# Even classes of a folded token transform folded once more: two 256x256 matrices in place of one 512x512, in a spectral filter block with its gradients

## The chip, the cores and the metric

The kernel runs on one core of a Trainium2 chip. The metric is the device time of one execution in microseconds (us). Engines are called by the profile's names: PE is TensorE (matmul, and PEld its weight loads), DVE is VectorE, ACT is ScalarE, POOL is GpSimd, SP is SyncE, which issues transfers. The chip has fast working memory in 128 partitions (SBUF), accumulators that matmuls write (PSUM), and main memory (DRAM here).

## The reference: what is computed

One block of a network on x of 2048 tokens by 1024 channels, conditioned by a vector c, and all gradients of it for a given grad_out. In short:

```
mod = silu(c) @ w_mod                 # six rows: sa, ca, ga, sb, cb, gb
h   = layernorm(x) * (1 + ca) + sa
x   = x + ga * irfft2(rfft2(h) * (w_r + 1j * w_i))       # A
h   = layernorm(x) * (1 + cb) + sb
n   = layernorm(h)
x   = x + gb * (gelu_tanh(n @ w1 + b1) @ w2 + b2)        # B, 1024 -> 3584 -> 1024
```

A is a filter over both the token axis and the channel axis. Its gradient is a transform, a product with the conjugate weights and a transform back once more, so the program holds two spectral passes: one forward, one backward. The outputs are x and the gradients for x, w_r, w_i, w1, b1, w2, b2, c and w_mod.

## The kernel before, in words

**Transforms as matmuls.** A real transform of 2048 tokens is computed with cosine and sine matrices after folding. A chunk i (of four) holds four groups of 128 tokens: rows 128i and 1024 + 128i are loaded in order, their mirror images, 2047 - 128i and 1023 - 128i downwards, by row indices through POOL (`load_tok`, L126). `fold_tok` (L271) adds and subtracts the mirrored groups on DVE, which gives four classes: even and odd cosine (CE, CO), even and odd sine (SE, SO), each with 512 rows over the four chunks and a 512x512 matrix. `fold_d` (L260) does the same along the channels. `unfold_tok` (L288) and `unfold_d` (L277) undo it. All these are additions through one helper, `tt` (L173), so in the profile they stand on L173.

**One spectral pass** is `spectral_core` (L478), called forward at L742 and backward at L1309. Its stages:

- `s_fwd` (L467) for CE, SE, CO, SO: eight column tiles of a class, four matmuls each (128x128 weights, 512 moving columns, L472), evicted from PSUM to U by a copy (L647; forward either ACT or DVE as the scheduler chooses). The matrices of CE and SE are in tile smA, those of CO and SO in smB.
- eight `pair`s (L495): the transform along channels (matmuls pcs of 256 columns, L505), the product with w_r and w_i on DVE, into R.
- `s_inv` (L556): back along the token frequencies, again four matmuls of 512 columns for each of eight tiles of a class (pv, L565), evicted to V. CE and SE run after the sixth pair, CO and SO after the eighth; CE and SE use a matrix tile smi.
- four chunks: 32 matmuls po of 256 columns each (L630), eight to a class, evicted into o4, a part of the tile ct (L635, L637), then `consume` of this chunk.

`consume_fwd` (L726) unfolds the chunk, stores it (d_A), adds the gated result to x, normalizes twice and stores the normalized rows (d_n, L740) from its temporary, ct[:,1] for even chunks and ct[:,2] for odd ones. ct has four such parts. `consume_bwd` (L1184) unfolds, forms the layernorm's gradient and column sums (accCA), and writes the gradient of x.

**What runs beside it.** PE has other matmuls to fill the gaps. Forward it is `ph_part` (L678, L684): grad_out times w2 transposed, 896 matmuls pp of 512 columns in 14 groups, each group with a weight tile wt that SP transposes while loading (L301; two in turn). grad_out is transposed for it by PE (pt, L344) and evicted with a column sum (L347 DVE, L351 ACT); the result pho is evicted (L691, L694) and stored. After that come `z_block` (n times w1, pz, L802; gelu and its derivative on ACT and DVE into tiles hh), which loads the normalized rows transposed as n3T (L791), and `bo_pass` (hh times w2, pbo, L853). Then `pg_pass` (L950), the layernorm gradients, and the second fold, `fold_quarter` (L1094). Beside the backward pass run the gradients of w2 (gw2acc, L1075, which loads hh again) and, at the end, of w1 (gw1acc, L1266).

**What sets the order.** A scheduler that knows the dependences fixes one order per engine when the program is built. On the chip each engine goes through its list and waits where an operand is not there. Evictions have a raised priority (`tc.high_priority`), some instructions are bound behind others (`issue_after`), and z_block and bo_pass follow a plan list. PSUM is divided by tags: "s" with 2 buffers (pu, pv, half of po and pcs), "d" for the other half, "f" with 4 (pt, pp and the gradients).

SP carries, in the stretch after the forward transform, the loads of wt, the stores of d_n, the loads of x (xt) and of n3T, and then w1 and hh, one after another.

## Time and profile before

| what | value |
|---|---|
| median of three runs | 1461.49 us (1461.4 to 1465.73) |
| profiled execution: its own time | 1459.13 us |
| its span | 1457.3 us |
| mean granted PE clock | 0.992 |
| ACT busy | 752.2 us, 52% |
| POOL busy | 366.1 us, 25% |

The stretches of the span that the change touches, by the busy time of the engines in the trace:

| stretch, us | what PE does | PE | DVE | ACT |
|---|---|---|---|---|
| 0 to 128 | conditioning rows, transposes, first pp | 98.95 | 99.03 | 76.87 |
| 128 to 156 | s_fwd, forward | 27.68 | 0.96 | 18.61 |
| 190 to 206 | s_inv of CE and SE, pairs 7 and 8 | 15.60 | 13.58 | 11.05 |
| 218 to 231 | s_inv of CO and SO | 13.00 | 1.10 | 8.24 |
| 231 to 272 | po of chunks 0 to 2, pp | 39.11 | 39.22 | 26.61 |
| 1020 to 1049 | s_fwd, backward | 29.00 | 11.12 | 19.31 |
| 1144 to 1159 | s_inv of CE and SE | 15.00 | 11.74 | 9.32 |
| 1189 to 1206 | s_inv of CO and SO | 15.22 | 7.15 | 9.54 |
| 1206 to 1353 | po, consume, gw2 and gw1 beside | 142.61 | 133.97 | 63.89 |

How to read the profile: a group of instructions has the line of the kernel, engine, operation, output<-input tiles, partitions x elements with type and the count; behind the first bar the busy time in us and the mean of one in ns; behind the second the idle time of the engine just before them, and what ended it. A line of a timeline has start and length in us, then the same, with the idle time before it and its releaser in brackets. Matmuls overlap, so the mean of one is longer than the distance from one to the next; the distance is read from a timeline, by start times and counts.

The longest waits of PE were for the weight blocks of the conditioning rows (12.4 us over six times, all before 100 us), for the eviction of the transposes (4.6), for evictions of po (3.9 on ACT, 1.1 on DVE), for R in s_inv (3.0) and for a wt tile (2.6, once).

### The profile page before, as it was taken

To read this page: it belongs to the slowest core of one execution; us is meant where nothing else is said; L and a number is where in the kernel's file an instruction comes from. 1 tells how busy PE (TensorE), PEld (TensorE's weight loads), DVE (VectorE), ACT (ScalarE), POOL (GpSimd) and SP (SyncE) were. 2 spreads that over 40 slices of the span, in tenths; PEclk is the share of its full clock that TensorE was granted. 3 is DMA by queue.
4 is the path that set the end of the run, shared out by engine and by line. 5 is a ranking of instruction groups with operands and counts; after the bars stand their busy time and mean duration, and the time that the engine had idled before them with its cause. 6 is when DMAs were issued, how large, how long until landed. Compare 5 with 4: busy or idle time off the path is not lost. (4 is left out here: it accounts for less than half of the span.)

```text
span 1457.3 us, 18411 instructions
## 1 busy us (share of the span) xinstructions
PE 1396.5 (96%) x6835; PEld 649.0 (45%) x6835; DVE 1058.4 (73%) x1483; ACT 752.2 (52%) x1065; POOL 366.1 (25%) x441
## 2 busy tenths in 40 slices
PE   5889999999999999999999999999999999999997
...
GB/s 333 286 214 70 142 235 115 270 255 337 257 203 278 259 250 233 201 264 241 277 297 245 74 271 185 107 270 176 181 217 254 254 233 213 194 191 180 297 279 65
DMA packets 358367, 324.28 MB, mean 223 GB/s; under 512 B 209386, under 2 KB 301056, under 8 KB 358022
## 3 DMA queue, kind: packets, MB, share of 16 engines
...
## 5 line engine op out<-in xcount | busy, mean ns | idle before, releaser
L684 PE MATMUL pp<-gBoT,wt 128*128 128x512 bf16 x896 | 197.9, 380 | 4.5 <-DMA wt<-in_B_w_dram 2.6
L950 PE MATMUL pg<-w1T,gzr 128*128 128x512 bf16 x896 | 197.1, 381 | 0.2 <-ACT gn3b L961 0.2
L1266 PE MATMUL gw1acc<-gzh,n3n 128*128 128x512 bf16 x896 | 195.4, 379 | 1.3 <-DMA gzh<-d_gz 1.3
L684 PEld LDWEIGHTS <-wt 128*128 128x128 bf16 x896 | 87.7, 98 | 109.4 <-issue 4.2
L950 PEld LDWEIGHTS <-gzr 128*128 128x128 bf16 x896 | 87.3, 98 | 108.7 <-issue 6.6
L802 PEld LDWEIGHTS <-w 128*128 128x128 bf16 x896 | 87.3, 98 | 108.8 <-issue 4.7
L1266 PEld LDWEIGHTS <-n3n 128*128 128x128 bf16 x896 | 87.4, 98 | 106.1 <-issue 2.7
L802 PE MATMUL pz<-n3Tb,w 128*128 128x512 bf16 x448 | 99.2, 379 | 1.6 <-DVE w2sD L875 1.4
L802 PE MATMUL pz<-n3Ta,w 128*128 128x512 bf16 x448 | 98.7, 379 | 1.1 <-ACT gt L805 1.1
L1075 PE MATMUL gw2acc<-gB,hhsA 128*128 128x512 bf16 x448 | 98.5, 379 | 1.0 <-DMA hhsA<-d_hh 1.0
L853 PEld LDWEIGHTS <-hhA 128*128 128x128 bf16 x608 | 59.0, 98 | 71.7 <-issue 1.4
L805 ACT ACTIVATE gt<-pz,b_col 128x512 bf16<-128x512 f32 x112 | 72.5, 684 | 34.2 <-PE pz L802 32.8
L1270 ACT CAST gwo<-gw1acc 128x512 bf16<-128x512 f32 x50 | 29.1, 583 | 113.6 <-PE gw1acc L1266 99.0
L173 DVE TENSOR_TENSOR gt<-gt,gt 128x2048 bf16<-128x2048 bf16 x56 | 68.3, 1223 | 22.4 <-ACT gt L813 21.2
L1082 ACT CAST gwo<-gw2acc 128x512 bf16<-128x512 f32 x46 | 26.7, 583 | 109.9 <-PE gw2acc L1075 75.6
L811 ACT ACTIVATE gt<-gt 128x2048 bf16<-128x2048 bf16 x28 | 53.5, 1910 | 55.7 <-DVE gt L173 55.7
L173 DVE TENSOR_TENSOR ct<-ct 128x2048 bf16<-128x2048 bf16 x64 | 75.9, 1218 | 1.8 <-DMA d_n<-ct 1.1
L1075 PEld LDWEIGHTS <-hhsA 128*128 128x128 bf16 x448 | 43.6, 98 | 53.0 <-DMA hhsA<-d_hh 1.7
L997 DVE CUSTOM_DVE_ANT_0 otl<-otl 128x1024 bf16<-128x1024 bf16 x24 | 29.1, 1223 | 49.9 <-DMA otl<-in_w_mod_dram 44.2
L807 ACT ACTIVATE gt<-gt 128x2048 bf16<-128x2048 bf16 x28 | 53.4, 1908 | 5.4 <-DVE hhC L173 2.5
L813 ACT ACTIVATE gt<-gt 128x2048 bf16<-128x2048 bf16 x28 | 53.5, 1909 | 0.5
L1271 POOL DMA_DIRECT2D out_dram<-gwo x56 | 30.6, 548 | 85.6 <-ACT gwo L1270 53.4
...
## 6 DMA issues: line engine op xcount, KB each, us to landing
...
```

The lines of the kernel that those rows point to most:

```text
L173: return nc.vector.tensor_tensor(out=out, in0=a, in1=b, op=op)
L684: last_pe[0] = nc.tensor.matmul(pp[:], lhsT=wt[:, fg % 2, cch, k * P:(k + 1) * P], rhs=gBoT[j][:, cch, :], start=(cch == 0), stop=(cch == ...
L802: last_pe[0] = nc.tensor.matmul(pz[:], lhsT=w1s[g][:, cch, k * P:(k + 1) * P], rhs=n3T[:, cch, :], start=(cch == 0), stop=(cch == NDC - 1))
L805: nc.scalar.activation(out=zb[:, k, :], in_=pz[:], func=ACT.Identity, bias=b1_col[:, fc:fc + 1], scale=1.0)
L807: nc.scalar.activation(out=av, in_=zb, func=ACT.Square)
L811: nc.scalar.activation(out=sg, in_=bv, func=ACT.Sigmoid, scale=2.0 * GK)
L813: nc.scalar.activation(out=bv, in_=bv, func=ACT.Sigmoid, scale=-2.0 * GK)
L853: last_pe[0] = nc.tensor.matmul(pbs[i][:], lhsT=hh[:, k, i * P:(i + 1) * P], rhs=wp[:, k, :], start=False, stop=(g == 6 and k == 3))
L950: last_pg[0] = nc.tensor.matmul(pgs[i][:], lhsT=gzs[b, g][:, k, i * P:(i + 1) * P], rhs=w1Ts[g][:, k, h * KH:(h + 1) * KH], start=(g == 0 ...
L1075: nc.tensor.matmul(acc[:], lhsT=hh_of(fc)[:, t, :], rhs=gBs[t // 4][:, t % 4, h * KH:(h + 1) * KH], start=(t == 0), stop=(t == NT - 1))
L1266: nc.tensor.matmul(acc[:], lhsT=n3ns[t // 4][:, t % 4, cch * P:(cch + 1) * P], rhs=gz2[t // 8][:, t % 8, :], start=(t == 0), stop=(t == NT ...
L1271: nc.gpsimd.dma_start(out=out_4[cch * P:(cch + 1) * P, fg * 512:(fg + 1) * 512], in_=ob)
```

## The change

The even classes are folded a second time over tokens. Chunk 2j + 1 no longer holds the tokens after those of chunk 2j but their mirror images about a quarter of the axis: rows 512 + 128j and 1536 + 128j in order, 511 - 128j and 1535 - 128j downwards by index (`tok_rows`, `tok_plain`, `tok_idx`). For the even classes, chunks 2j and 2j + 1 are added and subtracted (`fold_pair`, in place of `fold_d` in odd chunks). The sum needs only every other frequency, the difference the rest, so the 512x512 matrix of an even class becomes two of 256x256. The frequencies are ordered so that they stay apart: in s_fwd and s_inv each tile of CE and SE has two halves of 256 columns with two matmuls of 256 columns each, where it had four of 512 columns. CO and SO stay as they were, with their rows in the new order.

On the way back po of an even chunk takes both halves of the even classes for itself and for the odd chunk behind it: 48 matmuls and 12 evictions (16 matmuls for CO and SO, 32 for the halves), and the odd chunk 16 matmuls and four evictions, for CO and SO alone. The halves go to a tile eb; DVE adds them into this chunk's o4 and subtracts them into the next one's. Forward eb is ct[:, 1 + i % 2]; backward it is a tile of its own.

Besides: matrices, their generation and their copies in DRAM (d_SF, d_SI) become smaller for the even classes, smi takes four transposing loads instead of eight; w_r and w_i rows and their gradients follow the new order of frequencies with the same number of transfers; the transposes of grad_out become matmuls against the identity or a reversed identity with results in fp32, so that the reversal at pho's eviction goes; the row sa (saf) is added in odd chunks only, with factor 8 for 4; the column sum sacc takes a copy and an addition instead of a copy and three; backward all evictions of U, cs and V are ACT's, and PSUM tiles of the even classes there alternate between tags "s" and "f". The number of matmuls is 6835 before and after.

The diff, cut to its core:

```diff
@@ -123,45 +126,55 @@
     def tok_flat(ap):
         return ap[0] if len(ap.shape) == 3 else ap
 
+    def tok_rows(s3, i, lo, n):
+        step, base = (1024, 128 * (i // 2)) if i % 2 == 0 else (-1024, 1536 + 128 * (i // 2))
+        return bass.AP(tensor=s3.tensor, offset=s3.offset + base * D + lo, ap=[[D, P], [step * D, 2], [1, n]])
+
+    def tok_plain(t4, i):
+        return t4[:, 0:4:3, :] if i % 2 == 0 else t4[:, 1:3, :]
+
+    def tok_idx(i, q):
+        return 1 + q if i % 2 == 0 else 3 * q
+
     def load_tok(t4, src, i, eng=None):
         s3 = tok_flat(src)
-        ins = (eng or nc.sync).dma_start(out=t4[:, 0:4:3, :],
-                          in_=bass.AP(tensor=s3.tensor, offset=s3.offset + 128 * i * D, ap=[[D, P], [1024 * D, 2], [1, D]]))
+        ins = (eng or nc.sync).dma_start(out=tok_plain(t4, i), in_=tok_rows(s3, i, 0, D))
         for q in range(2):
-            nc.gpsimd.indirect_dma_start(out=t4[:, 1 + q, :], out_offset=None, in_=s3,
+            nc.gpsimd.indirect_dma_start(out=t4[:, tok_idx(i, q), :], out_offset=None, in_=s3,
...
@@ -267,6 +283,20 @@
         dv = dst.rearrange("p c (a b w) -> p c a b w", b=2, w=256)
         tt(dv[:, :, :, 0, :], tv[:, :, :, 0, :], tv[:, :, :, 1, :], ALU.add)
         return tt(dv[:, :, :, 1, :], tv[:, :, :, 0, :], tv[:, :, :, 1, :], ALU.subtract)
+
+    def fold_pair(dst, prev, src, tmp, spare):
+        n = 4
+        fwd = src.rearrange("p c (b w) -> p c b w", w=512)[:, :, :, 0:256]
+        rev = bass.AP(tensor=src.tensor, offset=src.offset + 1023, ap=[src.ap[0], [D, n], [-512, 2], [-1, 256]])
+        tv = tmp.rearrange("p c (s b w) -> p c s b w", s=2, w=256)
+        tt(tv[:, :, 0], fwd, rev, ALU.add)
+        tt(tv[:, :, 1], fwd, rev, ALU.subtract)
+        for c0, out in ((0, spare), (1, dst[:, 1:4:2, :])):
+            dv = out.rearrange("p c (a b w) -> p c a b w", b=2, w=256)
+            tt(dv[:, :, :, 0, :], tv[:, c0:4:2, :, 0, :], tv[:, c0:4:2, :, 1, :], ALU.add)
+            tt(dv[:, :, :, 1, :], tv[:, c0:4:2, :, 0, :], tv[:, c0:4:2, :, 1, :], ALU.subtract)
+        tt(dst[:, 0:4:2, :], prev[:, 0:4:2, :], spare, ALU.subtract)
+        return tt(prev[:, 0:4:2, :], prev[:, 0:4:2, :], spare, ALU.add)
 
     def fold_tok(h4, tmp):
...
@@ -339,9 +369,11 @@
         nc.vector.tensor_copy(out=gb_col[:], in_=pc[:, 0:NDC])
     for j in range(4):
         for cch in range(NDC):
-            pt = psum.tile([P, BW], BF16, tag="f", name="pt", bufs=4)
+            pt = ps_f("pt")
             for a in range(4):
-                nc.tensor.transpose(pt[:, a * P:(a + 1) * P], gos[j][:, a, cch * P:(cch + 1) * P], ident[:])
+                q = (0, 2, 3, 1)[a] if j % 2 == 0 else (1, 3, 2, 0)[a]
+                nc.tensor.matmul(pt[:, q * P:(q + 1) * P], lhsT=gos[j][:, a, cch * P:(cch + 1) * P], rhs=(ident, irev)[a // 2],
+                                 start=True, stop=True)
             if cch % 2 == 0:
                 with tc.high_priority():
...
@@ -467,10 +506,16 @@
     def s_fwd(cl, fb, sm, evac):
         Ut = reg.tile([P, 8, 512], BF16, name=f"U{cl}", tag=f"uv{cl}")
         for c8 in range(8):
-            pu = ps_s("pu")
-            for i in range(4):
+            pu = (ps_f if cl % 2 == 0 and c8 % 2 and fb is not fbuf else ps_s)("pu")
+            for i in range(4 if cl % 2 else 0):
                 last_pu[0] = nc.tensor.matmul(pu[:], lhsT=fb[:, i, cl, c8 * P:(c8 + 1) * P], rhs=sm[:, i, :],
                                               start=(i == 0), stop=(i == 3))
+            for k in range(0 if cl % 2 else 2):
+                cols = slice(k * 256, (k + 1) * 256)
+                for j in range(2):
+                    i = 2 * j + (k if cl == CE else 1 - k)
+                    last_pu[0] = nc.tensor.matmul(pu[:, cols], lhsT=fb[:, i, cl, c8 * P:(c8 + 1) * P], rhs=sm[:, j, cols],
+                                                  start=(j == 0), stop=(j == 1))
             with tc.high_priority():
                 evac(Ut[:, c8, :], pu[:])
...
@@ -560,10 +607,12 @@
                 dc, h = c8 // 2, c8 % 2
                 k0 = (0, 1, 2, 1)[dc] + 256 * h
                 base = k0 + (PW if (dc >= 2) == (cl < 2) else 0)
-                pv = ps_s("pv")
+                pv = (ps_f if cl % 2 == 0 and c8 % 2 and not fwd else ps_s)("pv")
                 for m in range(4):
-                    nc.tensor.matmul(pv[:], lhsT=R[:, cl * 4 + m, :, :].rearrange("p x w -> p (x w)")[:, base:base + 255:2],
-                                     rhs=smi[:, cl // 2, m, :], start=(m == 0), stop=(m == 3))
+                    k = (m // 2 + cl // 2) % 2
+                    out, m0, m1 = (pv[:], 0, 3) if cl % 2 else (pv[:, k * 256:(k + 1) * 256], m // 2 * 2, m // 2 * 2 + 1)
+                    nc.tensor.matmul(out, lhsT=R[:, cl * 4 + m, :, :].rearrange("p x w -> p (x w)")[:, base:base + 255:2],
+                                     rhs=smi[:, cl // 2, m, :], start=(m == m0), stop=(m == m1))
                 with tc.high_priority():
                     evac_v(Vt[:, c8, :], pv[:])
 
@@ -575,11 +624,11 @@
         smis = []
 
         def load_smi():
-            smi = reg.tile([P, 2, 4, 512], BF16, name="smi", tag="sma")
+            smi = reg.tile([P, 2, 4, 256], BF16, name="smi", tag="sma")
             for t in range(2):
                 with tc.issue_after(ld_in[0].ins):
                     if fwd:
-                        for i in range(4):
+                        for i in range(2):
                             nc.sync.dma_start_transpose(out=smi[:, t, :, i * P:(i + 1) * P], in_=d_SF[:, 2 * t, i, :])
                     else:
...
@@ -618,24 +667,34 @@
             nc.vector.tensor_scalar(out=gm[:, 8:12, :], in0=gm[:, 4:8, :], scalar1=-1.0, scalar2=None, op0=ALU.mult)
         ct = reg.tile([P, 4, 4, D], BF16, name="ct", tag=o4tag)
         xts = [reg.tile([P, 4, D], BF16, name="xt", tag=tg)[:] for tg in ("sma", "smb" if fwd else "px0")]
+        eb = None if fwd else reg.tile([P, 4, D], BF16, name="eb", tag="smb")[:]
         for i in range(4):
-            o4 = ct[:, 3 * (i % 2)]
-            for cl in range(4):
+            o4, on = ct[:, 3 * (i % 2)], ct[:, 3 - 3 * (i % 2)]
+            if fwd:
+                eb = ct[:, 1 + i % 2]
+            half = [(cl, eb[:, 2 * k + cl // 2], k * 256 + i // 2 * P) for cl in (CE, SE) for k in range(2)]
+            for cl, ov4, c0 in (half if i % 2 == 0 else []) + [(cl, o4[:, cl], i * P) for cl in (CO, SO)]:
                 for hh_ in range(2):
                     po = (ps_d, ps_s)[hh_]("po")
                     for d2 in range(2):
                         dc = 2 * hh_ + d2
                         for h in range(2):
                             gi = 2 * dc + h + (4 if (dc >= 2 and cl >= 2) else 0)
-                            nc.tensor.matmul(po[:, d2 * 256:(d2 + 1) * 256], lhsT=Vs[cl][:, 2 * dc + h, i * P:(i + 1) * P],
+                            nc.tensor.matmul(po[:, d2 * 256:(d2 + 1) * 256], lhsT=Vs[cl][:, 2 * dc + h, c0:c0 + P],
                                              rhs=gm[:, gi, :], start=(h == 0), stop=(h == 1))
                     with tc.high_priority():
-                        ov = o4[:, cl, hh_ * 512:(hh_ + 1) * 512]
+                        ov = ov4[:, hh_ * 512:(hh_ + 1) * 512]
                         if fwd or (cl, hh_) != (3, 0):
                             nc.any.tensor_copy(out=ov, in_=po[:])
                         else:
                             last_po[0] = nc.scalar.copy(out=ov, in_=po[:])
-            consume(i, o4, ct[:, 1 + i % 2], ct[:, 2 - i % 2], xts[i % 2])
+            if i % 2 == 0:
+                tt(o4[:, 0:4:2, :], eb[:, 0:2, :], eb[:, 2:4, :], ALU.add)
+                if fwd:
+                    tt(on[:, 0:4:2, :], eb[:, 0:2, :], eb[:, 2:4, :], ALU.subtract)
+            elif not fwd:
+                tt(o4[:, 0:4:2, :], eb[:, 0:2, :], eb[:, 2:4, :], ALU.subtract)
+            consume(i, o4, ct[:, 1 + i % 2], ct[:, 2 - i % 2], xts[i % 2], eb)
 
     def new_pair_temps(tags):
...
@@ -686,12 +745,8 @@
             q = (0, 2, 3, 1)[j]
             ov = ph2[:, :, q * P:(q + 1) * P]
             pv = pp[:, :].rearrange("p (i w) -> p i w", w=P)
-            if j % 2 == 0:
-                with tc.high_priority():
-                    nc.any.tensor_copy(out=ov, in_=pv)
-            else:
-                with tc.high_priority():
-                    nc.any.tensor_copy(out=ov, in_=bass.AP(tensor=pv.tensor, offset=pv.offset + 511, ap=[pv.ap[0], [-P, 4], [-1, P]]))
+            with tc.high_priority():
+                nc.any.tensor_copy(out=ov, in_=pv)
         if js[-1] == 3:
             nc.gpsimd.dma_start(out=d_ph[fc * P:(fc + 1) * P, :], in_=ph2.rearrange("p i w -> p (i w)"))
...
@@ -718,12 +773,16 @@
         norm_act(fb, x4, 0, i)
         tt(fb, fb, bcn(opca_row, 4), ALU.mult)
         fold_tok(fb, x4)
-        fold_d(fb, fb, x4[:])
-        tt(fb[:, 0, :], fb[:, 0, :], saf, ALU.add)
+        if i % 2 == 0:
+            fold_d(fb, fb, x4[:])
+        else:
+            pv_ = fbuf[:, i - 1]
+            fold_pair(fb, pv_, fb, x4[:], x4s[i - 1][:, 0:2, :])
+            tt(pv_[:, 0, :], pv_[:, 0, :], saf, ALU.add)
     css = reg.tile([P, 2, 2, 2 * PW], BF16, name="cs01", tag="px0")
     nc.gpsimd.memset(css[:], 0.0)
 
-    def consume_fwd(i, o4, tmp, tmp2, x4):
+    def consume_fwd(i, o4, tmp, tmp2, x4, eb):
         unfold_d(o4, tmp)
         unfold_tok(o4, tmp)
...
@@ -1093,7 +1152,10 @@
 
     def fold_quarter(b, ftmp, g2):
         fold_tok(ftmp, g2)
-        fold2_in[b] = fold_d(fbuf2[:, b], ftmp, g2)
+        if b % 2 == 0:
+            fold2_in[b] = fold_d(fbuf2[:, b], ftmp, g2)
+        else:
+            fold2_in[b] = fold_pair(fbuf2[:, b], fbuf2[:, b - 1], ftmp, g2, ftmp[:, 0:2, :])
 
     for b in range(NB):
...
@@ -1181,12 +1243,12 @@
     nc.gpsimd.memset(css2[:], 0.0)
     accCA = []
 
-    def consume_bwd(i, o4, tmp, tmp2, n1):
+    def consume_bwd(i, o4, tmp, tmp2, n1, eb):
         if i == 0:
             accCA.append(ps_s("accCA"))
-            nc.vector.tensor_copy(out=sacc, in_=o4[:, 0, :])
-        else:
-            tt(sacc, sacc, o4[:, 0, :], ALU.add)
+            nc.vector.tensor_copy(out=sacc, in_=eb[:, 0, :])
+        elif i == 2:
+            tt(sacc, sacc, eb[:, 0, :], ALU.add)
         unfold_d(o4, tmp)
         unfold_tok(o4, tmp)
...
@@ -1307,14 +1369,14 @@
                     next(rows34)
 
     spectral_core(False, fbuf2, (smA2, smB2), em2, [css2[:, 0], css2[:, 1]],
-                  new_pair_temps(["t0", "t1", "t2", "t3"]), act_copy, s_copy, act_copy, consume_bwd, "fr", pfs, fill, mid_bwd, beside_bwd)
+                  new_pair_temps(["t0", "t1", "t2", "t3"]), s_copy, s_copy, s_copy, consume_bwd, "fr", pfs, fill, mid_bwd, beside_bwd)
 
 
     accSA = [ps_d("accSA0"), ps_d("accSA1")]
     colsum(accSA, sacc, True, True)
...
```

## The prediction

> **What bounds the kernel now.** I read the page's busy shares first, then the groups of instructions of the even classes, then TensorE's waits, then the timelines of the four stages that the change touches.
>
> ```profile
> PE 1396.5 (96%) x6835; PEld 649.0 (45%) x6835; DVE 1058.4 (73%) x1483; ACT 752.2 (52%) x1065; POOL 366.1 (25%) x441
> ```
>
> TensorE (PE) is busy for 96% of the span: time taken from its stream is gained unless a wait takes its place. The even classes are two groups, with their weight loads and a group of half-width matmuls beside them:
>
> ```profile
> L472 PE MATMUL pu<-smA,fbuf 128*128 128x512 bf16 x128 | 28.5, 379 | 0.6 <-DVE fbuf L173 0.6
> L565 PE MATMUL pv<-smi,R 128*128 128x512 bf16 x128 | 28.4, 379 | 1.4 <-DVE R L173 1.2 <-ACT V L647 0.2
> L472 PEld LDWEIGHTS <-fbuf 128*128 128x128 bf16 x256 | 24.9, 98 | 31.4 <-DVE fbuf L173 1.1 <-issue 0.6
> L505 PE MATMUL pcs<-empf,U 128*128 128x256 bf16 x128 | 15.3, 273 | 0.0
> ```
>
> The 379 ns of one matmul is latency, not spacing. Spacing comes from PE's timeline at the start of the backward transform:
>
> ```profile
> 1018.64 2.11 PE L1075 MATMUL gw2acc<-gB,hht 128*128 128x512 bf16 x9
> 1020.58 14.00 PE L472 MATMUL pu<-smA,fbuf 128*128 128x512 bf16 x64
> 1034.51 0.61 PE L196 MATMUL acc3b<-au,ones_bf 128*32 128x512 bf16 x8
> 1048.88 1.91 PE L505 MATMUL pcs<-empf,U 128*128 128x256 bf16 x16
> 1050.63 0.59 PE L1075 MATMUL gw2acc<-gB,hhsA 128*128 128x512 bf16 x2
> ```
>
> (34.51 - 20.58)/64 = 0.2177 us for 512 columns; (50.63 - 48.88)/16 = 0.109 us for 256. Half the columns, half the time; the weight load of 98 ns still fits under it.
>
> **What goes.** s_fwd and s_inv, forward and backward, run 64 even-class matmuls each: 256, all from 512 to 256 columns; their number stays. 256 x (0.2177 - 0.109) = 27.8 us, 13.9 in each transform. The products at L630 stay 256 (48, 16, 48, 16 by chunk in place of 32 each).
>
> The Trainium skill, "TensorE: Matmul & The Clock Gate", Back-to-back issue gap, speaks against this: in streams of weight loads and matmuls it gives about 131 ns for 512 columns and 81 for 128. By it 256 matmuls could lose no more than 256 x 0.05 = 12.8 us, an estimate from the page. This trace disagrees at 512 columns, with 217.7 ns.
>
> **Forward, what comes.**
>
> (a) The fold before the first pu. fold_pair does four 128x2048 and four 128x1024 operations where fold_d did four 128x2048. VectorE's chain runs without a gap from 115.67 to 128.27 and PE already waits 0.6 us for it; a 128x1024 add takes 0.68 (0.61 back to back): 2.5 us more. PE comes 1.1 us earlier, having done a few even tiles before, and that waits too: +2.5 to 3.6, taken 3.
>
> (b) Evictions. An even tile now takes PE 4 x 0.109 = 0.44 us, its eviction on ScalarE 0.585, through two PSUM buffers. One tile per 0.6 to 0.66 us costs 16 x 0.2 = 3.2 us in s_fwd; the instruction order of the new program puts 18 single pcs matmuls (2.0 us) in the gaps: +1.3. s_inv likewise, with fewer fillers: +1.5. Bounds: 0 and 3.2 each.
>
> (c) The wait for d_n(0). The even halves of chunk 2 are evicted into ct[:,1], the temporary of consume(0), which is free only when the store of d_n(0) has landed. Before, in time:
>
> ```profile
> 270.28 2.05 ACT L635 CAST ct<-po 128x512 bf16<-128x512 f32 x4 [1.56 <-DMA d_A<-ct]
> 288.02 1.17 SPq L740 DMA_DIRECT2D d_n<-ct  x1
> 295.49 1.23 DVE L173 TENSOR_TENSOR ct<-ct 128x2048 bf16<-128x2048 bf16 x1 [0.56 <-DMA d_n<-ct]
> ```
>
> Chunk 2's evictions started at 270; the store was issued at 288.02, as soon as ScalarE's normalization ended, and landed at 295.4, 64.7 us after the first po at 230.7. Now chunk 0 needs 16 more matmuls and four more evictions (some 2 us) and two VectorE operations of 1.15 on the half-classes: about 70 us. PE's order up to chunk 2's second part is 72 po and 254 pp: 72 x 0.109 + 254 x 0.2177 = 63 us. So PE stands about 8 us; errors of 3 us on each side make it 2 to 14. In front of d_n(0) on SP stand two weight transposes; the later needs pp 640 done, 7 us before PE gets there, so it does not hold the store. Behind the waiting evictions stand, on ScalarE, the pp evictions and normalizations of chunk 1; on VectorE, the normalization sums; PE waits for the pp buffers. The same line, waiting for another store, cost PE 1.2 us at 270.92; that and 0.69 at 252.38 vanish: -1.9.
>
> The Trainium skill, same page, specification table, calls ScalarE's and VectorE's queues strictly first in, first out. The row agrees: at 270.28 pp evictions waited behind the copies for 1.56 us.
>
> (d) SP. The last weight transpose stays queued behind d_n(1). Issued at 314.9, its kind made PE wait 2.6 us at 330.05. PE's lead on it grows by a few us: +1.4, between -2.6 and +6.
>
> (e) z and bo. The normalizations of chunks 1 to 3 come some 6 to 12 us later against PE, into a stretch where ScalarE has little room:
>
> ```profile
> 272.00:350.00 78.00, 75.39 (x354) 34.45 (x353) 72.38 (x114) 50.09 (x78) 9.95 (x15) 1.00 0.95 286
> 350.00:410.00 60.00, 58.88 (x276) 26.45 (x275) 42.78 (x56) 54.19 (x55) 9.07 (x12) 1.00 0.82 269
> ```
>
> (Columns: stretch, length, PE, PEld, DVE, ACT, POOL busy, clock, DMA share, GB/s.) The hh tiles that bo reads were ready 8 to 16 us ahead (hh(0,1) at 383.1, used at 396.1): that slack hides it, but for a taken 0.6; bounds 0 and 12.
>
> Forward: -13.9 + 3 + 1.3 + 1.5 + 8 - 1.9 + 1.4 + 0.6 = 0.0.
>
> **Before 100 us** PE waits for weight blocks (12.4 us); fewer index and sine steps (ScalarE 2 x 1.14) lie beside that. Transposes as plain matmuls read fp32 PSUM at eviction: between ScalarE's 585 ns and VectorE's 688, against 683 and 743 now. Zero, plus or minus 1.
>
> **Backward, what comes.** Fold: VectorE's last operation ends at 1020.49, the first pu starts at 1020.58, and PE's order ahead is fixed: four halves and a gate-gradient step between, +2.5 to 3.7, taken 3.
>
> ```profile
> 1018.14 2.35 DVE L173 TENSOR_TENSOR fbuf<-gn3a 128x2048 bf16<-128x2048 bf16 x2
> 1027.69 0.59 ACT L647 CAST U<-pu 128x512 bf16<-128x512 f32 x1 [0.28 <-PE pu L472]
> ```
>
> Evictions: ScalarE had 0.28 us idle in each 0.86; two buffer sets now alternate, so a tile goes at 0.53 to 0.585 against 0.44, partly buffered: +1 in s_fwd, +0.5 in s_inv (0 to 2.3 each). gw2's loads of hh already end two waits (0.96 and 1.34 us at 1120.9 and 1138) with the DMA engines near 0.9 busy; PE comes 3 us earlier: +1, between 0 and 3. Consume: VectorE is busy 134 of 147 us from 1206 to 1353 and gets four operations of 1.15 for two sums of 0.68; the column sums accCA had 4 to 11 us slack: +1, 0 to 3. From 1352 only gw1's 448 matmuls follow, so what PE gained by then reaches the end. Backward: -13.9 + 3 + 1 + 0.5 + 1 + 1 = -7.4.
>
> **Sum.** 1459.1 (this execution) - 7.4 = 1451.7. The median of the three runs is 2.4 above that execution: **1454**.
>
> **Rivals.**
> - **Kept saving** (25%): the store lands as PE arrives, so (c) is nil, and (d) and (e) too. For: 8 us is the difference of two paths of 63 and 70 us, and an eighth off the longer removes it. Against: both its added operations stand on it. -7.4 - 8 - 1.4 - 0.6 = -17.4: 1444.
> - **Gain eaten** (21%): (c) at 12, hh loads at 3, consume at 2: -7.4 + 4 + 2 + 1 = -0.4, 1461. For: three supply chains already end waits of PE; PE comes earlier to all of them.
> - **Slower** (18%), one mechanism: the evictions of chunk 2 hold ScalarE's order until d_n(0) is stored, so the normalizations of chunks 1 to 3 slide into 350 to 410, where ScalarE has 5.8 us free in 60. Up to the 13 us by which hh(0,1) was early nothing shows; beyond that each us is one of PE at bo. Slid by 25 us, 12 of them count: -7.4 + 12 = +4.6, 1466. It decides at about 21 us of slide. Against: I count 6 to 12.
> - **No cheaper** (1%): the weight loads, 98 ns each, set the spacing, and the even classes gain nothing: -7.4 + 27.8 = +20.4, 1482. The pcs row speaks against it: 0.109 with a new weight load for each. The page weighed above would be its rule; by its figures 15 us of the 27.8 are lost: 1469.
>
> **How the numbers follow.** My forecast, 1449 to 1457, has 35%; with the kept saving that is 0.60 for faster by over 0.3% (below 1457.1; 0.3% is about what a measurement of this kernel can tell from no change), 0.21 within, 0.19 slower. Range 1440 to 1467: the kept saving with (a) and (b) at low ends, and the slower case.
>
> **What would show it.** Right: even-class matmuls 0.109 us apart where evictions don't pace them; pu waiting 3 to 4 us for fbuf in both transforms; one wait of po for ct, some 8 us near 290, released by d_n's store; the first z near 344; the first backward pu as early as forward gave (0), the last po some 4 to 5 us earlier, the end 7. Wrong: no wait of po there (kept saving), or pbo waiting for hh after 395 (slower). What I could not see is how long the store of d_n(0) takes among earlier weight transposes.

## The result and the profile after

The changed kernel is slower: 1478.5 us median (1471.0 to 1484.1, six runs) against 1462.6 us for the kernel before in the same session, a ratio of **1.0102 [1.0064, 1.0141]**; run again later, 1.0119 [1.009, 1.0149]. The profiled execution took 1477.05 us, its span is 1475.1, 17.8 us longer than before's 1457.3. The first line of the page, then two groups of the feed-forward products (busy time and mean ns of one, then idle time before them and what ended it):

```profile
PE 1378.1 (93%) x6705; PEld 651.9 (44%) x6835; DVE 1075.7 (73%) x1501; ACT 749.3 (51%) x1065; POOL 368.9 (25%) x446
...
L861 PE MATMUL pz<-n3Ta,w 128*128 128x512 bf16 x440 | 99.5, 384 | 16.0 <-ACT gt L864 15.7
L1134 PE MATMUL gw2acc<-gB,hhsA 128*128 128x512 bf16 x438 | 99.4, 384 | 4.6 <-DMA hhsA<-d_hh 4.0
```

PE works less (93% where it was 96%; some matmul records are missing, x6705 of 6835) and the program still ends later. Where it stands idle, from the view of PE's waits, four lines of the kernel before and then the changed kernel (total, times, longest, in us):

```profile
PE pv L565 <- DVE R L173: 3.0, 2, 1.8
PE pz L802 <- ACT gt L805: 1.3, 2, 1.1
PE gw2acc L1075 <- DMA hhsA<-d_hh: 1.0, 1, 1.0
PE pu L472 <- DVE fbuf L173: 0.6, 1, 0.6
```

```profile
PE pz L861 <- ACT gt L864: 15.9, 3, 12.3
PE pm L269 <- DMA wblk<-in_w_mod_dram: 10.2, 4, 3.9
PE pu L517 <- DVE fbuf L186: 6.5, 2, 5.9
PE pv L614 <- DVE R L186: 6.1, 2, 5.1
PE pp L743 <- DVE pho L749: 5.8, 1, 5.8
PE acc3a L209 <- DVE gn3a L1101: 4.1, 2, 3.8
PE gw2acc L1134 <- DMA hhsA<-d_hh: 4.0, 2, 2.5
PE po L683 <- ACT ct L688: 3.6, 1, 3.6
PE gw2acc L1134 <- DMA otl<-d_hh: 2.7, 1, 2.7
```

Against before, those for gt and R have grown most, with those for fbuf and hh (the one for pho lies at 79 us, ahead of the transforms). To place them I took one PE instruction at each stage's border and compared its start in the two executions (of the last matmul its end). PE's order at these borders is the same, so the differences add up. Minus is time won in a stretch, plus is time lost; beside each stand the same for a second execution of the changed kernel (changed_again) and the terms of the prediction that belong there:

| stretch, up to | before, us | after, us | after - before | change in this stretch | the same in the second execution | predicted |
|---|---|---|---|---|---|---|
| first z (pz<-n3Ta) | 343.9 | 332.3 | -11.6 | -11.6 | -10.5 | -13.9 + 3 + 1.3 + 1.5 + 8 - 1.9 + 1.4 = -0.6 |
| first pz<-n3Tb | 421.9 | 426.7 | +4.8 | **+16.3** | **+16.6** | +0.6 |
| start of gw2 | 964.2 | 972.9 | +8.7 | +3.9 | -1.6 | 0 |
| backward pu, odd class | 1035.1 | 1044.6 | +9.5 | +0.9 | -3.8 | -6.95 + 3 + 1 = -2.95 |
| backward pv, even class | 1144.9 | 1162.7 | +17.8 | **+8.3** | **+10.9** | +1 |
| backward pv, odd class | 1189.9 | 1201.3 | +11.4 | -6.4 | -2.8 | -6.95 + 0.5 = -6.45 |
| backward po | 1205.6 | 1223.0 | +17.4 | **+6.0** | **+5.4** | 0 |
| last matmul | 1449.6 | 1467.3 | +17.8 | +0.4 | +6.9 | +1 |

The three losses in bold are there in both executions; the other rows differ by up to 6.5 us between the two and are read with that in mind.

**Forward.** PE's timeline (start, length, engine, line, product, count, and in brackets the idle time before it and what ended it):

```profile
290.80 7.07 PE L683 MATMUL po<-gm,V 128*128 128x256 bf16 x48 [3.57 <-ACT ct L688]
332.31 7.07 PE L861 MATMUL pz<-n3Ta,w 128*128 128x512 bf16 x32
390.11 8.64 PE L861 MATMUL pz<-n3Ta,w 128*128 128x512 bf16 x31 [12.31 <-ACT gt L864]
405.60 6.85 PE L861 MATMUL pz<-n3Ta,w 128*128 128x512 bf16 x31 [3.40 <-ACT gt L864]
```

Most of the saving has arrived at 332.31 (11.6 of 13.9 us), and is gone at 390. What stands in front of the eviction gt, on ScalarE and then VectorE:

```profile
375.93 1.28 ACT L466 ACT_TABLE_LOAD   x1
382.35 0.30 ACT L466 ACTIVATE mv<-mv,eps_c 128x4 f32<-128x4 f32 x1 [5.14 <-DVE mv L477]
382.67 1.28 ACT L870 ACT_TABLE_LOAD   x1
385.31 1.91 ACT L870 ACTIVATE gt<-gt 128x2048 bf16<-128x2048 bf16 x1 [1.36 <-DVE gt L186]
387.13 2.36 ACT L500 ACTIVATE ct<-ct,stats 128x1024 bf16<-128x1024 bf16 x2
389.39 2.39 ACT L864 ACTIVATE gt<-pz,b_col 128x512 bf16<-128x512 f32 x4
```

```profile
370.35 2.29 DVE L186 TENSOR_TENSOR ct<-ct,rows 128x4096 bf16<-128x4096 bf16 x1 [6.44 <-ACT ct L500]
```

The gt evictions, which free PE's accumulators, stand in ScalarE's order behind the square root (L466) and the normalizations (L500) of a later chunk of x. That square root waits 5.14 us for VectorE's sums; in the kernel before it waited for nothing:

```profile
376.21 0.30 ACT L427 ACTIVATE mv<-mv,eps_c 128x4 f32<-128x4 f32 x1
```

My reading is that the later chunks are late because the evictions of chunk 2's products come late, and ScalarE and VectorE work the chunks off at their own rate whatever PE saved. On ScalarE these evictions begin so:

```profile
290.17 2.05 ACT L688 CAST ct<-po 128x512 bf16<-128x512 f32 x4 [0.90 <-DMA d_n<-ct]
```

ScalarE stood 0.90 us for the store of d_n(0); until 289.27 it was at the normalizations of chunk 1, which the order laid down for this program puts ahead of these evictions. So the shared tile can act in two ways, by the wait for the store and by the order; the experiments below change both together.

**Backward.** PE's timeline again:

```profile
1035.72 8.36 PE L517 MATMUL pu<-smA,fbuf 128*128 128x256 bf16 x63 [5.87 <-DVE fbuf L186]
1116.78 8.77 PE L1134 MATMUL gw2acc<-gB,hhsA 128*128 128x512 bf16 x31 [2.51 <-DMA hhsA<-d_hh]
1154.11 8.77 PE L1134 MATMUL gw2acc<-gB,otl 128*128 128x512 bf16 x31 [2.73 <-DMA otl<-d_hh]
1162.72 7.58 PE L614 MATMUL pv<-smi,R 128*128 128x256 bf16 x64
1207.21 1.46 PE L614 MATMUL pv<-smB,R 128*128 128x512 bf16 x3 [5.14 <-DVE R L186]
```

64 even-class matmuls take 7.58 us at 1162.72, where 64 of 512 columns took 14.0: the halves are as cheap as forecast. Four of these five stretches begin with a wait, and those of the first three lines are also long for their count. In the second and third, one record of 32 is missing (one step between two starts is double, 0.433 us): 32 matmuls of 512 columns take 8.77 us, elsewhere (332.31) 7.07.

That length is the clock: in the second line the steps between starts are 0.427 us until 1120.3 and 0.216 from then on, and from 1117.0 to 1120.3 the granted clock was 0.50. The same two stretches of the span in the two kernels, before first (stretch, length, busy us of PE, PEld, DVE, ACT, POOL, granted clock, DMA share, GB/s):

```profile
300.00:450.00 150.00, 146.10 (x679) 65.76 (x677) 130.53 (x167) 117.16 (x130) 21.60 (x30) 1.00 0.91 268
...
1060.00:1220.00 160.00, 155.92 (x793) 77.12 (x792) 110.93 (x153) 60.99 (x100) 67.44 (x79) 1.00 0.93 244
```

```profile
300.00:450.00 150.00, 133.29 (x603) 59.74 (x613) 126.43 (x160) 114.80 (x124) 19.72 (x27) 0.97 0.84 256
...
1060.00:1220.00 160.00, 147.33 (x732) 73.63 (x743) 105.80 (x150) 52.24 (x92) 67.33 (x77) 0.96 0.91 216
```

The granted clock was 1.00 in both stretches before, and 0.97 and 0.96 after; over the span 0.992 and 0.980. The lower line shows one thing more: the DMA engines are as busy (0.91 for 0.93) and move less, 216 for 244 GB/s.

### The profile page after: what moved, and what is told of

It reads as the page before. It is cut to its first block, busy times and chain, and to the rows that moved or that the text cites. A ratio compares the mean times of both kernels' runs of the same rounds, so it can differ in the third digit from the quotient of the medians.

```text
span 1475.1 us, 18310 instructions
## 1 busy us (share of the span) xinstructions
PE 1378.1 (93%) x6705; PEld 651.9 (44%) x6835; DVE 1075.7 (73%) x1501; ACT 749.3 (51%) x1065; POOL 368.9 (25%) x446
## 5 line engine op out<-in xcount | busy, mean ns | idle before, releaser
L1009 PEld LDWEIGHTS <-gzr 128*128 128x128 bf16 x896 | 87.3, 98 | 109.4 <-issue 7.2
L1328 PEld LDWEIGHTS <-n3n 128*128 128x128 bf16 x896 | 87.2, 98 | 107.8 <-issue 3.8
L861 PE MATMUL pz<-n3Ta,w 128*128 128x512 bf16 x440 | 99.5, 384 | 16.0 <-ACT gt L864 15.7
L186 DVE TENSOR_TENSOR ct<-ct 128x2048 bf16<-128x2048 bf16 x68 | 80.5, 1220 | 0.6
L749 ACT CAST pho<-pp 128x512 bf16<-128x512 f32 x62 | 35.8, 582 | 45.9 <-PE pp L743 45.2
```

Of the source, the lines that this page charges most:

```text
L186: return nc.vector.tensor_tensor(out=out, in0=a, in1=b, op=op)
L749: nc.any.tensor_copy(out=ov, in_=pv)
L861: last_pe[0] = nc.tensor.matmul(pz[:], lhsT=w1s[g][:, cch, k * P:(k + 1) * P], rhs=n3T[:, cch, :], start=(cch == 0), stop=(cch == NDC - 1))
L1009: last_pg[0] = nc.tensor.matmul(pgs[i][:], lhsT=gzs[b, g][:, k, i * P:(i + 1) * P], rhs=w1Ts[g][:, k, h * KH:(h + 1) * KH], start=(g == 0 ...
L1328: nc.tensor.matmul(acc[:], lhsT=n3ns[t // 4][:, t % 4, cch * P:(cch + 1) * P], rhs=gz2[t // 8][:, t % 8, :], start=(t == 0), stop=(t == NT ...
```

## The experiments

Each is compared with the kernel before on the same chip in the same session (its median there lay between 1464.2 and 1467.3 us). The stage times are of one profiled execution each; two of the changed kernel differ by nearly 9 us at one border (+9.8 and +1.1 at the first backward pcs), so verdicts go by the ratios, and stage times only tell where. An edit can also make the scheduler lay down other orders; where the traces show that it did, the text says so. "The pairs stretch" is the time from the first backward pcs to the first backward pv: 96.0 us before, 104.0 in the changed kernel, 106.5 in its second profile. Exchanged row orders (before_new_rows, changed_old_rows, own_eb_old_rows) put the filter's weights at other frequencies than the reference does; the instructions are the same.

**What is PE's time in a transform worth?** Four kernels take it away from the one or give it back to the other. Two leave out half of the even matmuls of the kernel before, and so save as many PE us as the split does (the same edit stands in s_inv):

```diff
-            for i in range(4):
+            for i in ((0, 3) if cl % 2 == 0 and fb is fbuf else range(4)):
```

> The kernel before, with two of the four matmuls of every even-class tile left out in the forward pass (s_fwd and s_inv), so that PE loses the same 13.9 us as by the change and nothing else is altered. Rival (time taken from PE forward reaches the end, and what the change adds takes it back): 1462 - 14 = 1448. Theory (the stretch from the first pz to bo is set by ScalarE and VectorE, which come no earlier): PE's waits there grow by most of what was taken, gain of 0 to 5, 1457 to 1462.

Measured: 1.0007 [0.9986, 1.0027]. 13.9 us less of PE work, and no gain. The first z starts 6.4 us early, and the wait that takes it back is in the profile, where the kernel before had 1.3 us in total:

```profile
PE pz L802 <- ACT gt L805: 6.3, 2, 5.0
```

The cut isn't the only difference, though. From the forward transform to 461 us ScalarE's order differs from that of the kernel before in 33 places and VectorE's in 49, and nine evictions went from ScalarE to VectorE. What is priced is the cut with the order that the scheduler made for it.

> The changed kernel with every even-class matmul of the forward pass done twice, which gives its 13.9 us back to PE there. If the forward saving is worth nothing (as before_cut_fwd has it), the time is that of changed_again within 4 us and PE's wait for gt near 378 shrinks by 10 us or more. If it is worth its length, 10 to 14 us slower.

```diff
-                for j in range(2):
+                for j in (0, 1) * (2 if fb is fbuf else 1):
```

Measured: 1.0126 [1.0102, 1.0151], with the 13.9 us given back to PE as good as equal to the changed kernel (1.0102 and 1.0119). The wait at pz is 3.5 and 2.9 us in place of 12.3 and 3.4, somewhat less of a fall than the 10 us expected. Here too the forward orders are others (35 places on ScalarE, 40 on VectorE).

> The changed kernel with every even-class matmul of the backward pass done twice, which gives the 13.9 us back to PE there and alters nothing else. Theory (the backward saving is swallowed by the wait for the fold, for hh and for R): slower than the changed kernel by 0 to 5 us, 1478 to 1483. Rival (the saving is in the time, and the loss lies elsewhere): 1492.

```diff
-                for j in range(2):
+                for j in (0, 1) * (2 if fb is not fbuf else 1):
```

Measured: 1.0111 [1.0082, 1.014]: equal to the changed kernel again. This is the clean one of the four: PE's, ScalarE's and VectorE's orders are those of the changed kernel, and on SP and POOL one pair of stores each has changed places near 1195 us. So 13.9 us of PE's time are worth nothing that can be measured in the backward transform of the changed kernel; in the forward one, and in that of the kernel before, the same holds for cut or addition together with the new order.

> The kernel before, with two of the four matmuls of every even-class tile left out in the backward pass, 13.9 us of PE. Rival (all of it reaches the end): 1448. Theory (the pairs are paced by transfers and VectorE: PE's waits for hh near 1120 and 1138 and for R near 1190 grow): 4 to 9 us gained, 1453 to 1458.

```diff
-            for i in range(4):
+            for i in ((0, 3) if cl % 2 == 0 and fb is not fbuf else range(4)):
```

Measured: 1.0135 [1.0108, 1.0162], but this kernel differs in more than the cut: the scheduler put evictions of U and V into VectorE's order, and PE stood 15.8 and 13.6 us for them. With these evictions held on ScalarE:

> before_cut_bwd again (two of the four matmuls of each even-class tile of the backward pass left out, 13.9 us of PE), but with all evictions of U and V on ScalarE, as the changed kernel has them, since in before_cut_bwd PE waited 16 and 14 us for two evictions that stood in VectorE's order. Theory (the saving backward is not reached by the end, because R and hh come no earlier): 2 to 7 us faster than before. Rival (it is): 12 to 14 us faster.

```diff
-                  new_pair_temps(["t0", "t1", "t2", "t3"]), act_copy, s_copy, act_copy, consume_bwd, "fr", pfs, fill, mid_bwd, beside_bwd)
+                  new_pair_temps(["t0", "t1", "t2", "t3"]), s_copy, s_copy, s_copy, consume_bwd, "fr", pfs, fill, mid_bwd, beside_bwd)
```

Measured: 1.0065 [1.0042, 1.0087], neither theory's number. A kernel with 13.9 us less for PE is slower, through these waits:

```profile
PE pcs L505 <- DVE rows L173: 14.6, 1, 14.6
...
PE pv L565 <- DVE R L173: 7.7, 2, 6.4
```

Here too the order moved: PE's first pcs now stands ahead of the odd classes' pu, and the 14.6 us are waited for there. So neither run says what the cut alone is worth in the backward transform of the kernel before.

**The forward loss: the tile of the even halves.** own_eb gives them a tile of their own (another buffer, free at that time) in place of the consumer's temporary, so that chunk 2 needn't wait for the store of d_n(0):

```diff
-        eb = None if fwd else reg.tile([P, 4, D], BF16, name="eb", tag="smb")[:]
+        eb = reg.tile([P, 4, D], BF16, name="eb", tag="px1" if fwd else "smb")[:]
...
-            if fwd:
-                eb = ct[:, 1 + i % 2]
```

> The changed kernel, but the even halves of the forward chunks go to a tile of their own and not to ct[:,1], so chunk 2's products need not wait for the store of d_n(0). Theory (the forward gain of 11.6 us at the first pz is lost because chunk 2's evictions, and with them the normalizations that the gelu evictions stand behind on ScalarE, start only when d_n(0) has landed): PE's wait for gt near 378 shrinks from 12.3 us to under 4, about 10 us less than the changed kernel, 1468 against 1478 (before 1462). Rival (that stretch is set by ScalarE's and VectorE's own work, wherever chunk 2 is evicted): the wait moves but does not shrink, within 3 us of 1478.

Measured: 1.0063 [1.0042, 1.0084], and of the waits for gt, where the theory said under 4 us and the longest is 5.0:

```profile
PE pz L859 <- ACT gt L862: 6.3, 2, 5.0
```

At the end of the forward part nothing is lost any more: the first pz<-n3Tb 0.3 us earlier than before (changed: 4.8 later), gw2's start 1.2 earlier (8.7 later). From the first z to pz<-n3Tb this kernel still loses 7.0 us (changed: 16.3), nearly as much as before_cut_fwd, which has no halves and no shared tile for them (7.6, with the same waits for gt). So some 9 of the 16 us go with the tile, and the other 7 come with a PE that is early. With the tile the scheduler also changed the orders between 200 and 466 us (31 places on ScalarE, 42 on VectorE); the run doesn't tell which part the wait for the store has and which the order. PE comes to the first backward pcs 4.4 us early, and then loses 11.7 in the pairs stretch (107.8) and waits 6.4 for R; the last matmul is 16.8 late. So there is a second loss, backward.

**The backward loss: five theories.** First, that the loads of row 5 of w_mod hold up what stands behind them on SP. These loads, with their sums and stores, were moved to the end, once in own_eb and once in the kernel before:

```diff
-    for _ in gmod_ring((5,), gmy, sacc):
-        pass
...
-    for r in (2, 1, 0):
+    for r in (5, 2, 1, 0):
```

> own_eb, and the gate gradient of row 5 (eight loads of w_mod on SP, sixteen VectorE operations, eight stores) moved from beside the last backward fold to the end of the kernel, beside gw1. Theory (backward, the saving is lost because the fold is late, and the loads of hh for the pairs stand on SP behind row 5's ring, which waits for VectorE until the fold is over): the wait of the first backward pu falls from 3 us to about 2, hhsA is issued some 10 us earlier against pu, the waits of gw2acc for hh fall from 7 us to under 3, the stretch from the first pcs to the first pv from 108 us to 98; 1477 becomes 1462 to 1468 where before is 1467. Rival (the pairs are bound by what the transfer engines move): the stretch stays at 104 to 108 and the time within 4 us of own_eb.

> The kernel before with the same move of row 5 to the end. Theory (before, fold and loads were just in time): no wait of PE goes but the 1 to 2 us for hh, within 4 us of the kernel before. Rival (the move helps any kernel): 8 us or more faster, as much as in own_eb.

Measured: 1.0077 [1.0054, 1.0101] and 0.9993 [0.9972, 1.0014]. In own_eb the wait for the fold shrank to 0.6 us and the first backward pcs came 8.4 us early, but the pairs stretch stayed at 106.6 and R was waited for 7.5 us. The theory falls: what is won ahead of the pairs is lost in them.

Then, that all the loads of w_mod in that stretch fill the DMA queues: without those of rows 3 to 5, which are made at the end.

```diff
-    rows34 = gmod_ring((3, 4), gmy, sacc)
...
-    for r in (2, 1, 0):
+    for r in (5, 4, 3, 2, 1, 0):
```

> own_eb with the gate gradients of rows 3 and 4 moved to the end too, which takes 16 loads, 16 stores and 32 VectorE operations from the pairs. Only the stretch of the pairs is read: if transfers bind it, the stretch from the first pcs to the first pv falls below that of own_eb_row5_late by 4 us or more and PE waits for neither hh nor R; if the row 5 ring alone delayed it, it is the same, 96 to 98. The end has 24 more steps beside gw1 and may be longer by 0 to 20 us.

Measured: 1.019 [1.0146, 1.0234], over four runs of which the profiled one was the fastest. The pairs stretch did fall to 99.9, the wait for R to 1.4 us, and the sums at the end of the transform (accSA) came 7.1 us early; but gw1's products then stood behind the moved loads:

```profile
PE gw1acc L1326 <- DMA gzh<-d_gz: 23.4, 4, 9.0
```

So what stands beside the pairs does set their stretch, but the move took 32 VectorE operations and 16 stores away with the 16 loads, and at the end there was no free place for them. Leaving out the loads of rows 3 and 4 altogether (their gradients are computed from what the buffer held), instead of moving them:

```diff
+            if r != 5:
+                return
```

> own_eb without the 16 loads of w_mod rows 3 and 4 in the pairs (the sums over them are formed from what the buffers hold, so the gradient for c is left out in part); their VectorE operations and stores stay. Theory (VectorE stands in each pair 3 to 6 us before such a load, which SP issues behind hh's, and this paces the pairs): first pcs to first pv falls from 108 to at most 101 us, PE's wait for R from 6.4 to under 3, the whole 8 to 14 us faster than own_eb. Rival (the volume of all transfers, or VectorE's own work, paces them): 104 or more, and 0 to 5 us faster.

Measured: 1.0093 [1.0059, 1.0127], pairs 103.5. No gain; this kernel waited 5.9 us for the fold and four times for hh in the pairs (7.9 us), and the volume of those loads alone isn't the cause.

Then, that d_P's loads stand on SP behind stores that POOL's scatters wait for; POOL issues them instead:

```diff
-                nc.sync.dma_start(out=pfs[n % 2].rearrange("p s r w -> p (s r w)"), in_=d_P[n])
+                nc.gpsimd.dma_start(out=pfs[n % 2].rearrange("p s r w -> p (s r w)"), in_=d_P[n])
```

> own_eb with the eight loads of d_P in the backward pairs issued by POOL and not by SP, so that SP's transposes of hh no longer stand behind a load that waits for a scatter. Theory (this queue carries the slower stores to PE): hh is issued some 4 us earlier in each pair, PE's waits for hh go from 7 us to under 2, first pcs to first pv from 108 us to at most 100, and the whole is 5 to 9 us faster than own_eb (1.0063), 0.999 to 1.003 of before; the wait for R may grow. Rival (hh is late because the transfer engines are full, whatever the queue): the stretch stays over 104 and the time within 3 us of own_eb.

> The kernel before with the same move of d_P's loads to POOL. Theory (its pairs were bound by PE, hh late by 2.3 us in all): 0 to 3 us faster than before. Rival (the move frees time in any kernel): 5 us faster or more.

Measured: 1.0102 [1.0075, 1.0129] and 1.008 [1.0058, 1.0102], pairs 110 and 108.6. Worse in both; this path isn't the way out.

The fifth theory looks at what the change does to the rows of w in DRAM. A load or a store of a w tile has 128 rows of 1026 bytes (513 bf16). Before, all went to every second row (2052 bytes apart); now those of the even classes (pairs 0 to 3) go to every fourth (4104 bytes apart), and those of the odd classes (pairs 4 to 7) still to every second, but in other blocks. The instructions, their counts and bytes stay. Each order was put into the other kernel, which leaves the orders of ScalarE, VectorE and of SP's transfers alone; of SP's waits one more stands in the backward pairs with the new rows, and it was over (1121.9) before SP came to it (1122.2):

```diff
-        return bass.AP(tensor=w.tensor, offset=w.offset + (256 * m + par) * DF, ap=[[2 * DF, P], [1, DF]])
+        base, step = ((1, 1025, 257, 1281)[m], 2) if par else (512 * (m % 2) + 2 * (m // 2), 4)
+        return bass.AP(tensor=w.tensor, offset=w.offset + base * DF, ap=[[step * DF, P], [1, DF]])
```

> The kernel before with the rows of w and of its gradients in the changed kernel's order, nothing else. Theory A: first pcs to first pv grows from 96 to 100 us to 102 to 106, 4 to 8 us slower than before. Theory B: no change, within 3 us.

> The changed kernel with the rows of w_r, w_i and their gradients loaded and stored in the order of the kernel before (every second row of 2048 in all pairs, in place of every fourth in pairs 0 to 3 and descending halves in pairs 4 to 7); the instructions and their order are the same, and the filter is applied to the wrong frequencies. Theory A (the new row order makes these transfers slower, and the ring of store, scatter and load in each pair waits for them): first pcs to first pv falls from 104 to 106.5 us to at most 100, and the whole is 5 to 10 us faster than changed_again (ratio 1.005 to 1.008). Theory B (the row order is without effect, the pairs lose time by the late loads after the fold): the stretch stays at 104 or more, ratio 1.009 to 1.014.

Measured: the kernel before with the new rows **1.0081 [1.0057, 1.0106]**, the changed kernel with the old rows **1.0058 [1.0038, 1.0078]** (changed: 1.0102 and 1.0119). The row order alone costs some 12 us in the one, more than theory A had, and about 6 to 9 in the other. The pairs stretch of the kernel before went from 96.0 to 109.4 (before_longer_fold, before_row5_late and before_cut_fwd, the kernel before with an edit elsewhere, have 97.4 to 100.2), that of the changed kernel from 104.0 and 106.5 to 102.3, not to the 100 of theory A. PE's timeline of the kernel before with the new rows:

```profile
1108.87 7.08 PE L1080 MATMUL gw2acc<-gB,hhsA 128*128 128x512 bf16 x31 [2.59 <-DMA hhsA<-d_hh]
...
1131.98 9.97 PE L1080 MATMUL gw2acc<-gB,hhsA 128*128 128x512 bf16 x32 [6.92 <-DMA hhsA<-d_hh]
1153.27 7.08 PE L1080 MATMUL gw2acc<-gB,otl 128*128 128x512 bf16 x31 [2.66 <-DMA otl<-d_hh]
```

And one stretch by windows, the kernel before first, then the same with new rows:

```profile
1050.00:1150.00 100.00, 97.70 (x496) 48.10 (x494) 72.36 (x102) 31.22 (x53) 46.15 (x53) 1.00 0.89 225
```

```profile
1050.00:1150.00 100.00, 89.78 (x443) 44.43 (x450) 63.32 (x89) 28.17 (x47) 40.93 (x45) 0.95 0.85 193
```

225 GB/s at a DMA share of 0.89 against 193 at 0.85: 253 and 227 GB/s for each unit of share. That isn't the rows' own packets: between the first pcs and the first pv those of 1026 bytes took 53 ns each in the kernel before and 54 with the new rows, while those of 256 bytes, of the transposing loads, took 25 and 28. Nor does this rate tell the two orders apart in other kernels (over the pairs stretch 237 in the changed kernel, 222 with the old rows). What does is how long SP's stores of w's gradients take from their issue until they have landed. The eight of pairs 0 to 3 take 4.6 to 5.0 us on average in the eight profiles with the old rows, and 5.4 to 6.1 in the nine with the new. For the six of pairs 4 to 6, whose rows stay 2052 bytes apart in both orders, it is 3.2 to 4.1 and 3.3 to 4.3 (once 5.5). Three profiles with fewer or otherwise issued transfers (own_eb_rows_late and the two with d_P on POOL) are left aside.

In the trace POOL's scatter waits for these stores, SP's load of d_P for the scatter, and the next transposing load of hh stands behind that load. In one pair the second store is issued at 1101.7, d_P's load at 1111.7 and hh's load at 1113.1 in the kernel before; with the new rows it is 1107.5, 1121.2 and 1122.7, 4 us more. PE's waits there are for these hh.

**The fold alone.** Four more 128x1024 VectorE operations (each a maximum of fbuf with itself) at the last backward fold of the kernel before:

```diff
+        for c in range(4 if b == NB - 1 else 0):
+            fold2_in[b] = tt(fbuf2[:, b, c, :], fbuf2[:, b, c, :], fbuf2[:, b, c, :], ALU.max)
```

> The kernel before with four more 128x1024 operations on VectorE at the end of the last backward fold (the maximum of a value with itself), as many as fold_pair adds. Theory B: the first backward pu waits 2.5 to 3.5 us, its first matmuls run at a lower clock, the hh loads of the pairs come later, and the stretch of the pairs grows by some us: 5 to 9 us slower than before in all. Theory A: only the wait itself, 2 to 4 us slower.

Measured: 1.0035 [1.0015, 1.0055], 4.2 us at the medians, and +4.8 at the last matmul of the profile. But 2.0 of these were there at the start of gw2 already, ahead of the edit (a wait of 2.30 us for w2sC at 731), and the first backward pu waits for nothing:

```profile
1022.55 14.01 PE L472 MATMUL pu<-smA,fbuf 128*128 128x512 bf16 x63
```

The four operations run from 1022.45 to 1024.93, beside the first pu, which begins with the chunks that they don't touch. So the run doesn't price the wait for a longer fold. The 2.8 us behind it come in the pairs and after; the waits for hh there are 3.4 us in place of 2.3.

**The clock.** The changed kernel once more, and with 140 matmuls of zeros ahead of its waits (into accumulators that are written anyway, adding nothing), so that PE stands still less (the first of the places; the others are alike):

```diff
+                for _ in range(14 if (fc, j, cch) == (20, 3, 7) else 0):
+                    nc.tensor.matmul(pp[:], lhsT=zero_bf[:], rhs=gBoT[j][:, 0, :], start=False, stop=False)
```

> The changed kernel once more, on the same chip as the next two, to be compared with them. Both theories: 1.007 to 1.014 of the kernel before.

> The changed kernel with 140 more matmuls against a block of zeros (30 us of PE), added into sums that PE holds anyway, just ahead of its longest waits: 14 ahead of chunk 2's second po, 44 and 12 beside the first bo steps, 24 before the backward pu, 26 before three waits for hh, 20 before the wait for R. Theory (each wait of PE of 2 us or more is followed by matmuls at a lower granted clock, 31 of them in 8.64 us where 7.07 is usual, and these add up to some 12 us): the matmuls after those places run at full clock, the mean clock goes from 0.977 to 0.985 or more, and the kernel is 3 to 8 us faster than the changed one although PE does more. Rival (the waits alone are the loss): no faster, or slower by up to 8 us where the added matmuls are longer than the waits.

Measured: 1.0119 [1.009, 1.0149] and 1.0088 [1.0061, 1.0115]: 1482.3 and 1478.1 us. With 30 us more work PE isn't slower but 4.2 us faster at the medians; the intervals overlap, so the size is uncertain and only "not slower" is safe. The granted clock was 0.972 to 0.978 in the runs of the one and 0.981 to 0.990 in those of the other. The added matmuls changed the orders as well (40 places on ScalarE, 65 on VectorE), and the waits for gt are nearly gone, so the clock isn't the only thing that differs.

**Both corrections.** The changed kernel with own_eb's tile and the old rows:

> The changed kernel with both single corrections: in the forward transform the even halves get a tile of their own instead of the temporary of the products' consumer, and the w rows stand in DRAM in the order of the kernel before. The matrices stay split. Theory (two independent losses, the buffer forward and the row order backward): the first z<-n3Ta about 7 us earlier and the gw2 start about 1 us earlier than in the kernel before, no pz wait of 12, the pairs stretch (first backward pcs to first backward pv of the even class) 98 to 102 us instead of own_eb's 107.8, ratio to the kernel before 0.998 to 1.003. Rival (the pairs stretch takes back whatever time PE brings to it, by supply that does not depend on the rows): first z and gw2 start the same, but pairs stretch 104 to 109, ratio 1.005 to 1.008.

Measured: 1.0033 [1.0014, 1.0052], between the two numbers, nearer to the theory. The stage times, one profile each, speak for it too: the pairs stretch is 97.8 us where own_eb had 107.8, and SP and the engines have the same orders in the two but for the rows. gw2 starts 1.6 us late, not 1 early. Differences to the kernel before, in us, at the borders of the first table:

| up to | changed | own_eb | changed_old_rows | own_eb_old_rows |
|---|---|---|---|---|
| first z | -11.6 | -7.3 | -12.2 | -6.3 |
| first pz<-n3Tb | +4.8 | -0.3 | +4.1 | +1.3 |
| start of gw2 | +8.7 | -1.2 | +2.7 | +1.6 |
| first backward pcs | +9.8 | -4.4 | +4.5 | +0.1 |
| backward pv, even | +17.8 | +7.3 | +10.8 | +1.9 |
| backward pv, odd | +11.4 | +1.6 | +6.5 | -3.7 |
| backward po | +17.4 | +10.0 | +14.1 | +5.0 |
| last matmul | +17.8 | +16.8 | +18.1 | +9.8 |

In the last column 1.9 us are lost up to 1147, and s_inv's saving arrives at the odd class, 3.7 us early. PE's timeline from there on, in the kernel before and then in this one:

```profile
1192.45 13.34 PE L565 MATMUL pv<-smB,R 128*128 128x512 bf16 x61 [1.78 <-DVE R L173]
```

```profile
1186.18 0.81 PE L612 MATMUL pv<-smB,R 128*128 128x512 bf16 x3
1194.58 16.21 PE L612 MATMUL pv<-smB,R 128*128 128x512 bf16 x61 [7.59 <-DVE R L185]
```

R comes when VectorE has worked off the last pairs, 2.1 us later than before; that PE was 3.7 early only makes the wait longer, and 2.9 us go in the slower matmuls behind it. A wait of 5.4 us for gz at the first gw1 product (1.25 before) and the slow matmuls after it are the next loss. No version with the halves beat the kernel before.

## Why the prediction was wrong

The forecast was 1454 us, faster; it came out at 1478, slower. Three steps failed: the premise that PE's saved time reaches the end, the term (e), and a term for the order of w's rows that isn't there. Point by point:

- **The saving per matmul** was right: 0.109 us at 256 columns. That s_inv's stretch gained 6.4 us where 6.45 were forecast is partly luck; in the second execution it is 2.8. The rival "no cheaper" is out.
- **What bounds the kernel**: this is the first step that failed. The prediction read 96% busy as "time taken from its stream is gained unless a wait takes its place" and then priced the waits that the diff makes. padded_bwd shows, with the orders unchanged, that 13.9 us given back to PE in the backward transform move nothing: waits for what other engines supply had taken their place. before_cut_fwd and padded_fwd say the same of the forward transform, there with new orders.
- **Forward (a) to (d)** were forecast at -0.6 together and measured at -11.6. The first pu waited 0.6, not 3; the evictions cost PE little; at chunk 2's evictions PE waited 3.6 where 8 were taken (the store's cover was 66 us, not 70, and ScalarE stood only 0.9 of it for the store); the transpose waited for at 330 was not waited for. Each stands on the cautious side, and what they left was lost in (e).
- **(e) z and bo** is the term of the sum that failed: 0.6 taken, bounds 0 and 12, measured +16.3. The mechanism is the rival "slower", with ScalarE's order and the sliding normalizations; it ended the matter at pz, whose evictions stand in that order, and not at pbo for want of hh as the rival had it. Its price was 12 us; there it took 15.7 of waits. With chunk 2's halves in a tile of their own (own_eb) 7.0 of the 16.3 us are left, as many as before_cut_fwd loses there without any halves (7.6). So the tile has some 9 of them, by the wait for the store or by the order that goes with it, and a PE that is early has the rest.
- **Middle, forecast 0**: +3.9, of which 2.1 are a wait for w2sC at 734.9 and 1.5 the slow matmuls after it; in the second execution -1.6, so this is no cause.
- **Fold, 3 taken**: PE waited 5.9 in the one execution and 2.8 in the second, so the 3 were about right and the rest is chance. The halves have gate-gradient operations of VectorE between them; in the first execution one of them came 4.95 us late at 1023, for a reason that the profile doesn't name (in the kernel before the same operation waited 2.77 us for row 5 of w_mod).
- **Pairs, hh +1**: +8.3. This is the third step: the prediction has no term for the order of w's rows, since the diff leaves the number and size of the transfers alone. It is worth 0.8% in the kernel before (before_new_rows, with the engines' orders unchanged), the largest single cause found; in the changed kernel it is 0.4 to 0.6%, in own_eb 0.3%.
- **R, no term**: +6.0. s_inv's saving met VectorE's last pairs.
- **The clock, no term**: part of each of the above. The sum of (1 - granted clock) x time from 100 us on is 4.6 us before and 22.1 after; of that, 1.7 and 15.2 lie where PE was busy.

Single causes don't add up to the 1.0%: row order 0.8 in the one kernel and 0.3 to 0.6 in the other, the tile of the halves about 0.25 to 0.4 (1.0058 to 1.0033, 1.0102 to 1.0063, with intervals that overlap), against savings of PE's time that bought nothing where they could be tried. That each loss takes up slack that another would have used is my reading, not a test.

**What stays open.** Why stores to rows four apart land later isn't shown, nor that the chain by way of scatter, d_P and hh is the only way from there to PE: the one change to it that was tried, d_P on POOL, made both kernels slower. Whether the tile acts by the wait for the store or by the new order is open too. And what is left of both corrections, 0.33%, was read in one trace (R, gz), not tested.
